# VectorE copies of K's indicator rows, and a last output block in two halves, in a chunk-select attention with a gMLP block

## The chip, the cores and the metric

The kernel runs on one core of a Trainium2 chip. Its engines work side by side and wait for each other through semaphores: TensorE (PE in the profile; its weight loads are PEld), VectorE (DVE), ScalarE (ACT), GpSimd (POOL) and SyncE (SP), which here only issues DMAs and waits. The metric is the device time of one execution in microseconds (us); lower is better. Times of one instruction are often given in nanoseconds (ns).

## The reference

Two layers follow each other. The first is a causal attention that lets every query attend to only six chunks of 32 keys, chosen by an upper bound of its scores; the second is a gMLP block over the 512 features of the eight heads together.

```python
def _attn_ref(q, k, v):                       # (4, 8, 768, 64) each
    k_min, k_max = min, max of k over chunks of 32 rows
    ub = sum_d maximum(q * k_min, q * k_max)   # (B, H, 768, 24)
    ub = where(causal, ub, -1e9)
    top_chunks = argsort(ub)[..., -6:]
    scores = q @ k.T / sqrt(64)
    mask = (chunk of key in top_chunks) & (query pos >= key pos)
    attn = softmax(where(mask, scores, -1e9))
    return attn @ v

def _moe_ref(x, w_in, g_ln, w_sg, b_sg, w_out):   # x (4, 768, 512)
    h = gelu_tanh(x @ w_in)                        # (4, 768, 1024)
    u, v = h[..., :512], h[..., 512:]
    v_n = layer_norm(v) * g_ln
    v_s = einsum('ts,bsd->btd', w_sg, v_n) + b_sg[None, :, None]
    return x + (u * v_s) @ w_out
```

Inputs and output are float32.

## The kernel before

**Stages.** The 32 heads are worked off as 16 pairs, four pairs to a batch of the gMLP. For a pair p, `prep(p)` transposes K and Q on TensorE (tags ktr and qtr, line 508), takes K's minimum and maximum by chunk on VectorE (kmm, L532), moves K and Q out of PSUM (kev, qev; L425 on ScalarE, L428 on VectorE), computes the upper bounds on TensorE (ub, L602 or L649), and finds the sixth largest on VectorE: transposes (utr), MAX8 (m8), a comparison (dn), a transpose back (dt). `scores` or `scores_full` computes the scores on TensorE (sc) with exp on ScalarE (exp) and the causal triangle on GpSimd (aff); `head` multiplies by V (pv, pvd) and divides on VectorE (rcp, xs, the latter into tile XS). `xtrans` transposes the result of a pair for the gMLP (xtr, and xev out of PSUM, into xT). After four pairs `moe_h` computes gelu of both halves (hv, gv; hu, gu) and the normalization (bns, bna, var, rstd, vhat), and `moe_g` the spatial product (pt, vs, gt), the output projection (ou, L926), the residual add on VectorE (os, L933) and the store (st, L937).

**How chunks that were not chosen are masked.** For the first four pairs the scores get extra matmuls with an indicator matrix (L763). For pairs 4 to 15 the indicator is part of the operands instead: a K operand `KA[w][i]` has 64 rows of K and 64 rows of an indicator (tile INDF, 128 x 768 in bf16), and `QA[w][i]` has 64 rows of Q and the mask rows that DMAs write (qd, L682). There are four such buffers (w = p mod 4). For pairs 4 to 7 `mask_rows(w)`, called after the scores of pair w, puts the indicator rows into the buffer that pair w has left: one DMA of 64 x 768 bf16 for each of the two heads (tag mrow, L690), and a memset of QA on GpSimd (L693). From pair 8 on (KSPR) the rows come by two other DMAs (kcp L545, kin L548), which the change leaves alone.

**The order of the work.** Every step is registered with `P.op(engine, fn, cost, tag, reads, writes, ...)` and gets the next number; from the names read and written the program derives what each step must wait for. The order on each engine is not that of the program but a list of these numbers (TABLE), found ahead of time by a search with the costs given to `P.op`; TensorE's list also says where spare matmuls are put in ("filler"), and "slots" gives each PSUM tile its bank. An engine works off its list strictly in order, so a step that waits holds up all that stand behind it in the same list; for SyncE these are DMA issues. DMAs of one name (`dma=`) wait for each other: an mrow DMA of one head waits for the one before to land.

Numbers that come up below: mrow 206 and 208 (pair 0), 258 and 260 (pair 1), 323 and 325 (pair 2), 375 and 377 (pair 3); the first of each two is for the head whose K rows are the lower ones and waits for the scores of its pair. ktr of pair 9: 578 and one more; qtr of pair 9: 589 and 591; load of half of K of pair 9: 411; of K of pair 12: 658 and 659; of half of Q of pair 12: 660 (a load of pair p overwrites the buffer of pair p − 3). kmm of pair 3: 152, 156, 157; qev of pair 3: 161. kev of pair 5, second half: 270, 271. dn and dt of pairs 4 and 5: 288, 289; wev, a move of transposed gMLP weights: 142. In the last batch ou, os and st of block 3 are 1288, 1289, 1290; of block 4 1291, 1292, 1293; of block 5 1294, 1295, 1296.

## Time and profile before

| what | value |
|---|---|
| median of 3 runs | 216.06 us (215.18 to 216.32) |
| the profiled execution | 216.26 us |
| its span, first to last instruction | 214.5 us |
| granted TensorE clock, mean | 0.999 of full speed |
| DMA | 35.47 MB, mean 165 GB/s |
| output stores (L937), issue to landing | 2.3 us, median of 24 |

The profile lists instructions by engine and by line of the kernel (L690 is line 690). "out<-in" are the tiles an instruction writes and reads. A row such as "6.4, 542 | 0.5 <-PE" means 6.4 us busy in all, 542 ns mean of one, and 0.5 us for which the engine was idle just ahead of these instructions, ended by TensorE. The chain of waits follows the execution back from its last instruction, at each step to what released it. SPq is SyncE's issuing of DMAs; a DMA's landing is told apart from its issue.

### The profile page before, as it was taken

The page shows a single profiled execution, that of the slowest core. Times are in us where ns is not written, and L with a number is a line of the kernel's source. Part 1 is how long each engine was busy: PE and PEld are TensorE (multiplying, and loading weights), DVE is VectorE, ACT ScalarE, POOL GpSimd, SP SyncE. Part 2 cuts the span into 40 slices and gives each one's busy share as a digit, 9 for nine tenths or more (in the row PEclk, how much of TensorE's full clock was granted, in tenths as well). Part 3 has the DMA queues.
Part 4 walks back from the last instruction along what each step waited for, and adds up shares of the span by engine and source line. Part 5 has one row for each costly group of instructions (what it writes and reads, how often), then busy time and mean ns, then how long its engine had stood idle before and what let it go on. Part 6 is the DMA issues. An engine that isn't in the chain of part 4 may idle for free.

```text
span 214.5 us, 5915 instructions
## 1 busy us (share of the span) xinstructions
PE 202.6 (94%) x2331; PEld 134.4 (63%) x2345; DVE 183.1 (85%) x526; ACT 149.9 (70%) x223; POOL 101.3 (47%) x151
## 2 busy tenths in 40 slices
PE   7789999879999999999999999999999999999993
PEld 2547668634766668697555676779445669545641
DVE  3599789979989998798899898988897877879983
ACT  2778997717798668988868777889868888353000
POOL 7346669965425948768260076399102542010000
PEclk9999999999999999999999999999999999999999
DMA  7999999999579998969987918848104402010316
GB/s 152 218 218 204 260 265 294 297 207 261 92 192 268 207 236 242 241 161 246 213 188 161 193 47 172 255 127 121 44 0 125 113 19 82 3 49 5 142 55 238
DMA packets 87450, 35.47 MB, mean 165 GB/s; under 512 B 80128, under 2 KB 82432, under 8 KB 87424
## 3 DMA queue, kind: packets, MB, share of 16 engines
q1 hardware_dynamic: 87424, 35.11, 70.9%
q8 instruction: 18, 0.29, 0.6%
q14 instruction: 8, 0.07, 0.1%
HBM read 24.77 MB, written 6.29 MB: 145 GB/s over the span
## 4 chain that ended last, share of the span: by engine, by line
PE 72%; DVE 11%; ACT 7%; DMA 4%; issue 2%; SPq 1%; POOL 1%; DVEq 0%
PE PSG L907 13%; PE PSC L717 12%; PE PSG L926 9%; PE PSG L844 7%; PE PSG L508 7%; PE PSG L795 6%; PE PSG L890 5%; DVE W L532 3%; ACT E L772 3%; PE PSG L649 3%; PE PSG L802 2%; DMA kn<-in_k_dram 2%; PE PSC L367 2%; PE PSG L829 2%; PE PSC L757 2%; ACT KA L425 2%
## 5 line engine op out<-in xcount | busy, mean ns | idle before, releaser
L723 ACT ACTIVATE E<-PSC 128x1024 bf16<-128x1024 f32 (+1 forms) x72 | 63.0, 920 | 9.3 <-PE PSC L717 8.0
L532 DVE TENSOR_REDUCE W<-PSG 128x12 f32<-128x384 f32 x64 | 32.8, 547 | 6.4 <-PE PSG L508 6.4
L717 PE MATMUL PSC<-QA,KA 128*128 128x128 bf16 (+2 forms) x336 | 37.5, 246 | 0.4 <-DMA QA<-Dt 0.3
L907 PE MATMUL PSG<-wsgT,vhat 128*128 128x384 bf16 x192 | 35.0, 326 | 0.0
L572 POOL CAST QA<-qT 64x768 bf16<-64x768 f32 (+1 forms) x28 | 23.0, 822 | 15.7 <-PE PSC L717 14.1
L728 POOL TENSOR_SCALAR_AFFINE_SELECT E<-E 128x768 bf16<-128x768 bf16 x24 | 20.6, 866 | 20.5 <-ACT E L723 20.2
L717 PEld LDWEIGHTS PSC<-QA,KA 128*128 128x128 bf16 x336 | 24.1, 98 | 7.5 <-issue 1.1
L895 ACT ACTIVATE uT<-PSG 128x384 bf16<-128x384 f32 x32 | 15.6, 491 | 17.5 <-PE PSG L890 17.2
L907 PEld LDWEIGHTS PSG<-wsgT,vhat 128*128 128x128 bf16 x192 | 18.0, 98 | 11.1 <-DVE PSG L913 0.5
L890 PE MATMUL PSG<-xT,winb 128*128 128x384 bf16 x128 | 23.9, 326 | 0.0
L848 ACT ACTIVATE vgb<-PSG 128x512 f32<-128x512 f32 x24 | 14.2, 597 | 13.9 <-PE PSG L844 13.0
L772 ACT ACTIVATE E<-PSC 128x1024 bf16<-128x1024 f32 (+1 forms) x24 | 20.6, 914 | 4.1 <-PE PSC L763 4.1
L913 DVE SCALAR_TENSOR_TENSOR PSG<-PSG,glnT,bsgbc 128x384 f32<-128x384 f32 x32 | 19.7, 619 | 3.8 <-PE PSG L907 3.5
L844 PE MATMUL PSG<-winb,xT 128*128 128x512 bf16 x91 | 21.4, 379 | 0.9 <-DVE xT L428 0.5
L926 PE MATMUL PSG<-woutb,uT 128*128 128x512 bf16 x87 | 21.6, 379 | 0.6 <-DVE rden L810 0.2
L795 PE MATMUL PSG<-vx,E 128*128 128x65 bf16 x480 | 19.9, 194 | 0.7 <-ACT E L772 0.7
L795 PEld LDWEIGHTS PSG<-vx,E 128*128 128x128 bf16 x480 | 17.6, 98 | 3.0 <-ACT E L772 0.9
L917 DVE TENSOR_TENSOR uT<-PSG,uT 128x384 bf16<-128x384 f32 x32 | 17.6, 553 | 1.2 <-ACT uT L895 0.3
L565 POOL TENSOR_SCALAR rT<-qT 128x576 f32<-128x576 f32 x16 | 10.9, 683 | 15.7 <-ACT qT L425 11.0
L812 DVE TENSOR_TENSOR XS<-PSG,rden 128x384 bf16<-128x384 f32 x32 | 17.5, 549 | 0.7
L933 DVE TENSOR_TENSOR osb<-PSG,XS 128x512 f32<-128x512 f32 x24 | 16.1, 684 | 2.0 <-PE PSG L926 1.9
L853 DVE BATCH_NORM_STATS2 stats<-vgb 128x6 f32<-128x512 f32 x24 | 15.7, 680 | 2.4 <-ACT vgb L848 2.3
(84 smaller groups left out, 339.9 us busy)
## 6 DMA issues: line engine op xcount, KB each, us to landing
qn<-in_q_dram SPq DMA_DIRECT2D x32, 192.0 KB, 4.7
kn<-in_k_dram SPq DMA_DIRECT2D x32, 192.0 KB, 4.6
vn<-in_v_dram SPq DMA_DIRECT2D x16, 384.0 KB, 5.0
out_dram<-osb SPq DMA_DIRECT2D x24, 256.0 KB, 2.3
uT<-in_moe_w_sg_dram SPq DMA_DIRECT2D x4, 384.0 KB, 4.8
KA<-INDF SPq DMA_DIRECT2D x16, 96.0 KB, 4.3
vgb<-in_moe_w_in_dram SPq DMA_DIRECT2D x3, 512.0 KB, 6.7
QA<-Dt SPq DMA_DIRECT2D x24, 36.0 KB, 2.3
```

The source lines that it names most:

```text
L532: P.op("dve", lambda d, m=m, op=op, src=src, h0=h0, h1=h1: d.tensor_reduce(W[w][:, m, 12 * h0:12 * h1].rearrange("p (h c) -> p h c", h=h1 ...
L572: P.op("pool", lambda g, i=i, r0=r0, r1=r1: g.tensor_copy(QA[w][i or 0][r0:r1, :], qT[r][r0:r1, :]), gps(S, 250 if i == 1 else 150), ("qca ...
L717: r = e.matmul(t.ap()[:, o:o + n], KA[w][i][:, 128 * kb:128 * kb + 128], QA[w][i][:, q0:q0 + n], start=True, stop=True)
L723: P.op("act", lambda e, t=t, c0=c0, c1=c1, i=i: e.activation(E[es][:, i, c0:c1], t.ap()[:, 0:c1 - c0], ACTF.Exp, scale=SCALE), act(c1 - c0 ...
L728: P.op("pool", lambda g, ev=ev: g.affine_select(ev, ev, pattern=[[0, NT], [1, 128]], compare_op=ALU.is_ge, fill=0.0, base=0, channel_multi ...
L772: P.op("act", lambda e, t=t, c0=c0, c1=c1, n=n: e.activation(E[es][:, :, c0:c1], t.ap().rearrange("p (i x) -> p i x", i=2)[:, :, 0:n], ACT ...
L795: r = e.matmul(t.ap()[:, 65 * qb:65 * qb + 65], E[es][:, i, a:a + 128], vx[w][:, kb, i, :], start=first, stop=False, skip_group_check=True)
L844: r = e.matmul(t.ap()[:, 0:F], xT[s][:, dk, 128 * qt:128 * qt + 128], winb[:, dk, F:DFF], start=(dk == 0), stop=(dk == NDK - 1))
L890: r = e.matmul(t.ap()[:, 0:TG], winb[:, dk, 128 * fb:128 * fb + 128], xT[s][:, dk, TG * tg:TG * tg + TG], start=(dk == 0), stop=(dk == NDK ...
L907: r = e.matmul(t.ap()[:, 0:TG], vhat[s][:, sb, 128 * fb:128 * fb + 128], wsgT[:, sb, TG * tg:TG * tg + TG], start=(sb == 0), stop=(sb == N ...
L913: P.op("dve", lambda d, t=t, fb=fb, tg=tg: d.scalar_tensor_tensor(t.ap()[:, 0:TG], t.ap()[:, 0:TG], glnT[:, fb:fb + 1], bsgbc[:, TG * tg:T ...
L926: r = e.matmul(t.ap()[:, 0:DM], gT[s][:, fb, 128 * qt:128 * qt + 128], woutb[:, fb, :], start=(fb == 0), stop=(fb == NF - 1))
```

## The change

Three things change. The two copies of INDF's rows in `mask_rows` are made by VectorE's `tensor_copy` (MROW = "dve") and no longer by DMAs; the names that they read and write stay. The residual add and the store of block 5 of the last batch, the last one in the program, are each split into two halves of 256 columns (LAST = 1), the second store under a DMA name of its own. And all lists of TABLE are new: the eight numbers of mrow have gone from SyncE's list to VectorE's, two numbers are new (1295 and 1296 are add and store of the first half, 1297 and 1298 of the second), and the other steps stand in another order on all five engines.

```diff
@@ -316,6 +316,8 @@
     VH = ("dve","dve","dve","dve")
     XDMA = tuple((2, d) for d in range(NDK))
     WSGT = "bf16"
+    MROW = "dve"
+    LAST = 1
     NWSB = 1
     TRX = 750
     TRI = 1300
@@ -687,9 +689,13 @@
 
         for i in range(2):
             m0 = 64 * (1 - i)
-            P.op("sp", lambda e, i=i, m0=m0: e.dma_start(KA[w][i][m0:m0 + 64, :], INDF[m0:m0 + 64, :]),
-                 dmac(590), ("mrow", w, i, 0), reads=["INDF"], dma=f"mrow{i}", xfer=450,
-                 writes=[("KI", w, i)] + ([("KA", w, 0, 0), ("KA", w, 0, 1)] if i == 0 else []))
+            ki = [("KI", w, i)] + ([("KA", w, 0, 0), ("KA", w, 0, 1)] if i == 0 else [])
+            if MROW == "dve":
+                P.op("dve", lambda d, i=i, m0=m0: d.tensor_copy(KA[w][i][m0:m0 + 64, :], INDF[m0:m0 + 64, :]), (290, 380),
+                     ("mrow", w, i, 0), port=True, reads=["INDF"], writes=ki)
+            else:
+                P.op("sp", lambda e, i=i, m0=m0: e.dma_start(KA[w][i][m0:m0 + 64, :], INDF[m0:m0 + 64, :]),
+                     dmac(590), ("mrow", w, i, 0), reads=["INDF"], dma=f"mrow{i}", xfer=450, writes=ki)
             P.op("pool", lambda g_, i=i, m0=m0: g_.memset(QA[w][i][m0:m0 + 64, :].bitcast(mybir.dt.uint32), 0),
                  gps(S // 2, 150), ("mrow", w, i, 2), shift=(i == 0), writes=[("QD", w, i)] + ([("QA", w, 0, 0), ("QA", w, 0, 1)] if i == 0 else []))
 
@@ -930,13 +936,19 @@
                      reads=[("uT", s, fb, tg) for fb in range(NF)] + [("woutb", fb) for fb in range(NF)],
                      writes=[t], alloc=t)
                 os_ = (b * NT + qt) % 3
-                P.op("dve", lambda d, t=t, qt=qt, os_=os_: d.tensor_tensor(
-                    osb[os_][:].rearrange("p (a x) -> p a x", x=128),
-                    t.ap()[:, 0:DM].rearrange("p (a x) -> p a x", x=128), XS[:, b % 2, :, qt, :], op=ALU.add), dve(DM), ("os", b, qt),
-                    reads=[t] + [("XS", b % 2, hh) for hh in range(H)], writes=[("osb", os_)], ps=[t])
-                P.op("sp", lambda e, qt=qt, os_=os_: e.dma_start(
-                    bass.AP(out.tensor, (b * S + 128 * qt) * DM, [[DM, 128], [1, DM]]), osb[os_][:]), dmac(),
-                    ("st", b, qt), reads=[("osb", os_)], dma=f"o{os_}", xfer=680)
+                cuts = (0, DM // 2, DM) if LAST and (b, qt) == (B - 1, NT - 1) else (0, DM)
+                for x, (c0, c1) in enumerate(zip(cuts, cuts[1:])):
+                    more = (x,) if len(cuts) > 2 else ()
+                    P.op("dve", lambda d, t=t, qt=qt, os_=os_, c0=c0, c1=c1: d.tensor_tensor(
+                        osb[os_][:, c0:c1].rearrange("p (a x) -> p a x", x=128),
+                        t.ap()[:, c0:c1].rearrange("p (a x) -> p a x", x=128), XS[:, b % 2, c0 // 128:c1 // 128, qt, :],
+                        op=ALU.add), dve(c1 - c0), ("os", b, qt) + more,
+                        reads=[t] + [("XS", b % 2, hh) for hh in range(c0 // 64, c1 // 64)],
+                        writes=[("osb", os_) + more] if more else [("osb", os_), ("osb", os_, 0), ("osb", os_, 1)], ps=[t])
+                    P.op("sp", lambda e, qt=qt, os_=os_, c0=c0, c1=c1: e.dma_start(
+                        bass.AP(out.tensor, (b * S + 128 * qt) * DM + c0, [[DM, 128], [1, c1 - c0]]), osb[os_][:, c0:c1]), dmac(),
+                        ("st", b, qt) + more, reads=[("osb", os_) + more] if more else [("osb", os_), ("osb", os_, 0), ("osb", os_, 1)], dma=f"o{os_}" if x == 0 else "olast",
+                        xfer=680 * (c1 - c0) / DM)
 
     SEL, GRP, u = {}, {}, 0
...
 TABLE = {
     "pe": (
...
-        "496 490 515 560 469 558 475 556 390 472 466 398 487 565 563 484 541 589 493 543 481 567 652 650 517 "
-        "478 530 512 591 505 578 519 502 534 526 624 527 522 523 582 617 621 499 574 626 575 674 597 628 619 "
...
+        "496 490 560 515 469 558 475 390 556 472 466 398 563 487 484 543 567 519 591 589 481 512 478 541 493 "
+        "652 650 565 578 530 517 505 502 624 526 527 534 617 522 523 582 621 499 626 574 575 674 597 628 619 "
...
-        "1261 1285 1253 1282 1270 1273 1267 1294 1291 1288 "),
...
+        "1241 1285 1253 1282 1270 1273 1267 1291 1294 1288 "),
...
     "dve": (
...
-        "97 163 153 156 117 157 25 118 200 161 119 120 201 204 205 211 212 168 169 170 256 171 257 216 217 26 "
-        "252 130 253 264 263 266 224 300 265 27 317 318 134 321 235 322 222 270 271 269 268 369 352 370 373 "
-        "374 274 417 276 424 282 425 285 283 286 284 287 420 380 381 421 432 428 433 138 429 440 436 142 441 "
-        "437 288 442 385 289 386 447 449 146 448 445 444 150 446 334 333 497 498 491 329 492 328 470 471 476 "
...
-        "1266 1277 1278 1262 1263 1286 1287 1283 1284 1271 1274 1268 1292 1295 1289 "),
...
+        "157 163 26 25 152 156 27 161 117 206 118 153 119 204 200 120 205 201 211 212 168 169 235 208 258 170 "
...
+        "370 268 274 417 276 270 271 375 323 424 285 286 282 380 287 425 420 381 283 421 284 428 432 429 288 "
+        "433 138 440 436 441 437 142 442 289 385 386 449 447 146 448 446 445 150 444 260 334 333 497 498 491 "
+        "328 492 329 470 471 476 477 473 467 474 468 402 399 403 400 488 404 489 485 401 482 405 325 377 406 "
...
+        "1281 1256 1257 1259 1265 1260 1277 1266 1262 1263 1286 1278 1287 1283 1284 1271 1274 1268 1292 1295 "
+        "1297 1289 "),
...
     "sp": (
-        "32 31 29 30 34 33 35 36 38 39 41 64 40 65 67 66 37 172 122 123 42 124 131 173 125 206 127 72 68 258 "
-        "75 121 73 174 175 70 295 294 135 231 323 139 297 232 375 143 178 296 208 147 230 99 229 290 347 98 "
-        "292 291 180 260 182 348 176 293 349 550 126 413 414 325 411 552 551 346 412 486 298 377 408 483 407 "
-        "233 480 410 611 613 409 612 538 507 549 350 610 504 722 586 607 661 660 609 553 501 859 721 608 539 "
-        "614 658 860 587 695 919 857 861 647 606 720 659 696 920 648 719 723 415 716 715 718 858 918 662 917 "
...
-        "921 1016 954 812 997 1083 1086 1089 1110 1104 1107 1272 1275 1269 1293 1296 1290 "),
...
+        "68 174 175 70 295 294 135 232 139 231 297 143 296 349 147 180 230 413 229 290 291 99 98 292 348 178 "
+        "412 176 293 182 298 347 346 414 126 551 552 660 411 486 233 410 408 483 407 480 549 613 409 661 612 "
+        "350 610 538 611 607 606 550 586 860 614 721 553 659 695 658 722 608 859 539 719 720 647 723 587 415 "
...
+        "1089 1104 1110 1107 1272 1275 1269 1293 1296 1298 1290 "),
...
     "filler": (
-        "54:9 43:1 81:2"),
+        "52:8 43:2 81:3"),
...
```

8 lines of the change are left out of this document (4 added, 4 removed), and 80 rows, old and new, of the table TABLE.

## The prediction, made before the changed kernel was run

> **What bounds the kernel now.** I read the page first: its span, its busy shares and the chain of waits.
>
> ```profile
> span 214.5 us, 5915 instructions
> PE 202.6 (94%) x2331; PEld 134.4 (63%) x2345; DVE 183.1 (85%) x526; ACT 149.9 (70%) x223; POOL 101.3 (47%) x151
> PE 72%; DVE 11%; ACT 7%; DMA 4%; issue 2%; SPq 1%; POOL 1%; DVEq 0%
> ```
>
> TensorE is busy for 94% of the span and holds 72% of the chain that ends last. The profiled execution took 216.26 us around its span of 214.5, so 1.76 us lie outside the span; the median of the runs shown is 216.06, which is 0.20 less. The sum below is made against 216.26.
>
> An average says little here, so I asked next for the busy time by stages.
>
> ```profile
> core 0: us, PE busy (x) PEld busy (x) DVE busy (x) ACT busy (x) POOL busy (x), PEclk, DMA share, GB/s
> 20.00:45.00 25.00, 22.59 (x451) 16.96 (x452) 22.05 (x71) 19.55 (x26) 19.90 (x29) 1.00 1.09 271
> 45.00:165.00 120.00, 117.93 (x1340) 79.50 (x1351) 108.10 (x331) 95.32 (x148) 62.97 (x87) 1.00 0.75 172
> 165.00:205.00 40.00, 39.84 (x359) 25.24 (x361) 33.40 (x69) 22.32 (x31) 7.92 (x9) 1.00 0.20 63
> ```
>
> From 45 to 205 us TensorE lacks only 2.07 + 0.16 us of 160. From 20 to 45 us it lacks 2.41 of 25, and there VectorE is busy for 22.05, idle for 2.95. Who ends that stage is in the chain of waits, followed through 38 to 46 us (start, length, what):
>
> ```profile
> 38.60 0.43 DVE xT L428
> ...
> 43.17 0.57 DVE XS L812
> ...
> 43.78 0.52 PE PSG L829 x6
> ...
> 44.89 0.47 DVE qT L428
> ```
>
> VectorE ends the stage: it finishes the fourth pair's output (XS), then moves its transpose (xT), and the gMLP's matmuls can begin. What shortens VectorE's list ahead of 45 us brings the filled stretch forward by as much; what lengthens it pushes that back. VectorE's own waits, and ScalarE's longest, between 20 and 45 us (total, times, longest):
>
> ```profile
> ACT E L772 <- PE PSC L763: 2.3, 4, 1.1
> DVE U L612 <- PE PSG L602: 1.6, 2, 1.0
> DVE rden L810 <- PE PSG L802: 0.7, 2, 0.5
> ```
>
> **The eight copies: their price.** The change takes eight DMAs of 96 KB (L690) off SyncE and gives VectorE eight copies of 64 partitions x 768 bf16, SBUF to SBUF. No row has such a copy. The nearest rows of VectorE, with those that the later steps need (groups by line and shape: busy, mean ns of one):
>
> ```profile
> L913 DVE SCALAR_TENSOR_TENSOR PSG<-PSG,glnT,bsgbc 128x384 f32<-128x384 f32 x32 | 19.7, 619 | 3.8 <-PE PSG L907 3.5
> L917 DVE TENSOR_TENSOR uT<-PSG,uT 128x384 bf16<-128x384 f32 x32 | 17.6, 553 | 1.2 <-ACT uT L895 0.3
> ...
> L933 DVE TENSOR_TENSOR osb<-PSG,XS 128x512 f32<-128x512 f32 x24 | 16.1, 684 | 2.0 <-PE PSG L926 1.9
> ...
> L428 DVE COPY xT<-PSG 128x768 bf16<-128x768 bf16 x12 | 6.4, 542 | 0.5 <-PE PSG L829 0.2
> ...
> L428 DVE CAST KA<-PSG 64x384 bf16<-64x384 f32 x4 | 2.2, 548 | 0.0
> ...
> L384 DVE MEMSET IND<- 32x768 bf16 x1 | 0.7, 698 | 0.1
> ...
> L364 DVE MEMSET warm<- 128x256 uint32 x1 | 0.3, 272 | 0.9 <-PEq L1118 0.9
> ```
>
> Above stands 0.70 us, one element at a time (L384). Below stands 0.27 us, the time of 256 words (L364). I take 0.41: 768 bf16 are 384 words of 32 bits, and 384 x 272/256 = 408 ns; the copy of as many elements out of PSUM takes 0.54.
>
> By the Trainium skill, "VectorE: DVE Perf Modes", section "The perf-mode tier table", a bf16 copy within SBUF runs at four elements a cycle, and its section on the TRN2 errata gives a measured fixed term of about 150 cycles; the estimate from these is (192 + 150)/0.96 = 356 ns, and with it the forecast would be 0.16 us lower. No row of this trace shows that mode.
>
> **Where the copies stand.** In the new list of VectorE three of them (206, 208, 258) stand ahead of the end of that stage, five after it. 206 and 258 wait for the last scores of pairs 0 and 1, which those stages of the list have behind them, so nothing queues up behind a wait. The two casts of K's second half of pair 5 (270, 271) go the other way, from ahead of pair 3's XS to behind qT's last move, into VectorE's wait for the first gelu. So the list ahead of the end of the stage becomes 3 x 0.41 = 1.23 longer and 2 x 0.548 = 1.10 shorter. The new list also puts three reductions and a qT move (157, 152, 156, 161) before the transpose that waited longest (1.0 of "DVE U L612"); I count that 1.0 as filled, and half of the 0.7 of rden, because two more ready instructions are put ahead of these reciprocals: −1.35. Stage: 1.23 − 1.10 − 1.35 = **−1.22**. The bounds: with copies at 0.27, −1.64; with copies at 0.70 and nothing filled, 2.10 − 1.10 = +1.00. The other five copies cost 5 x 0.41 = 2.05 us of VectorE after 45 us, where it is idle for 120 − 108.10 = 11.9; I take nothing. Two of them stand between the comparison and the transpose of pairs 6 and 7 (dn and dt of that group), but one vs (L913, 0.62) is moved out of the same place. Without that cover they cost 0.82.
>
> **SyncE's queue without the eight DMAs.** Here are L690's own instructions (min/median/max ns), and then SyncE's waits between 24 and 50 us:
>
> ```profile
> L690 SPq DMA_DIRECT2D KA<-INDF x8: 467/639/1586, 23.7 to 76.8; - x8
> DMA to landing us min/median/max: 2.8/4.5/6.9
> ```
>
> ```profile
> SPq L199 <- DMA KA<-INDF: 4.7, 2, 3.5
> SPq L690 <- PE PSG L802: 1.3, 1, 1.3
> ```
>
> Each of these DMAs waits for the one before of its name to land, so SyncE stood still for 4.7 us. That queue time is freed, and about 8 x 0.64 = 5.1 us of issuing. It is worth only what a late load cost TensorE; in the whole trace two places show a wait of TensorE on a DMA after the first loads:
>
> ```profile
> 60.69 0.51 PE L717 MATMUL PSC<-QA,KA 128*128 128x128 bf16 x6 [0.28 <-DMA QA<-Dt]
> ...
> 117.17 0.55 PE L508 MATMUL PSG<-identF,kn 128*128 128x128 f32 x3 [0.52 <-DMA kn<-in_k_dram]
> ```
>
> The second is K of pair 12. In the new list of SyncE its two loads (659, 658) stand ahead of the indicator DMAs of pairs 8 and 9 instead of behind them, some 20 entries earlier: **−0.52**. The first is the mask rows of pair 4: the new list of VectorE puts their comparison and transpose (288, 289) ahead of a copy of 0.55 us (142): **−0.28**. Bounds of both: 0 to what is taken.
>
> **What the new order makes late.** SyncE works its list in order. It now has 660, Q of pair 12, right ahead of 411, half of K of pair 9. 660 overwrites Q of pair 9 and must wait until TensorE has transposed both of its halves (591, 589). From there to 578, the transpose that reads 411, TensorE's new list holds two output blocks, one spatial block, two score tiles and three transposes. Prices from the chain of waits, and then the loads' issue (min/median/max, ns) and landing between 64 and 85 us:
>
> ```profile
> 61.74 0.66 PE PSG L508 x6
> ...
> 74.80 0.97 PE PSG L907 x6
> ...
> 76.10 0.86 PE PSG L926 x4
> ...
> 78.19 0.44 PE PSC L717 x4
> ```
>
> ```profile
> L492 SPq DMA_DIRECT2D qn<-in_q_dram x7: 583/686/2320, 64.6 to 84.8; - x7
> ...
> DMA to landing us min/median/max: 3.4/4.6/6.4
> ```
>
> TensorE: 2 x 0.86 + 0.97 + 2 x 0.44 (the smaller of the two tiles less, 0.3) + 3 x 0.33 = 4.4 us. SyncE: 0.69 + 4.6 = 5.3. K arrives 0.9 late; **+0.8** is taken for the wake-up that both share. From both sides: 0.69 + 3.4 gives nothing, 0.69 + 6.4 gives +2.7.
>
> **The tail.** The last microseconds, instruction by instruction:
>
> ```profile
> 209.14 1.67 PE L926 MATMUL PSG<-woutb,uT 128*128 128x512 bf16 x7
> ...
> 209.99 1.29 DVE L933 TENSOR_TENSOR osb<-PSG,XS 128x512 f32<-128x512 f32 x2 [1.04 <-PE PSG L926]
> 210.44 0.38 PE L926 MATMUL PSG<-woutb,uT 128*128 128x512 bf16 x1
> ...
> 211.20 0.68 DVE L933 TENSOR_TENSOR osb<-PSG,XS 128x512 f32<-128x512 f32 x1
> 211.31 0.93 SPq L937 DMA_DIRECT2D out_dram<-osb  x2
> ```
>
> Before, TensorE makes blocks 5, 4, 3 (1294, 1291, 1288) while VectorE adds 4, 5, 3 (1292, 1295, 1289): it idles for 1.04 us until block 4 is there and then has three adds of 0.68 in a row, the last from 211.20 to 211.88, though TensorE ended at 210.82. After, TensorE's list ends 1291, 1294, 1288. The block that is cut is number 5, which is last in the program and not on any engine: block 3 still ends everything, whole. Block 4's add begins one block earlier, at about 209.13; the halves of block 5 begin when it is done, at 209.99. A half costs 256 elements: from 384 elements at 0.553 (L917) and 512 at 0.684, 0.42 each, 0.84 for 0.68. They end at 210.83, when block 3 is there. Its add ends at about 211.52 instead of 211.88: **−0.36**. It comes from the order; the cut itself costs 0.16 of VectorE and one more issue (0.93 for two, so 0.47) on SyncE, which ends near 211.4, before the last add does. Bounds: 0 to −0.4.
>
> **Sum:** −1.22 − 0.52 − 0.28 + 0.80 − 0.36 = −1.58, so 216.26 − 1.58 = **214.7 us**.
>
> **The rivals.**
> *Stage ahead of 45 us unchanged* (216.0): the idle that the list fills at one place opens at the next, as VectorE waits for TensorE's scores anyway. 1.23 − 1.10 − 0.52 − 0.28 + 0.80 − 0.36 = −0.23. For it speaks that ScalarE, too, waited 2.3 us there; against it that VectorE alone stands in the chain.
> *The idle all filled* (213.1): 2.95 instead of 1.35 of VectorE's idle goes.
> *K of pair 9 at the slowest landing* (216.6): 2.7 instead of 0.8.
> *Copies held up by GpSimd* (slower). GpSimd is busy for 19.90 of 25 us in that stage, with instructions such as the first row; the second is a VectorE instruction that reads SBUF alone, with its shortest, median and longest time:
>
> ```profile
> L728 POOL TENSOR_SCALAR_AFFINE_SELECT E<-E 128x768 bf16<-128x768 bf16 x24 | 20.6, 866 | 20.5 <-ACT E L723 20.2
> ```
>
> ```profile
> L879 DVE TENSOR_SCALAR vhat<-vgb,mv,rstd x24: 529/542/636, 57.9 to 195.7; 128x512 bf16<-128x512 f32 x24
> ```
>
> If a copy costs 0.70 and waits out half of such an instruction (0.43), the three make 3 x 1.13 − 1.10 = +2.29, nothing is filled, the rest gives −0.36: 218.2. With p the price of a copy the time is 216.26 + 3p − 1.46, which passes 217.14 from p = 0.78. Against it: L879 takes 0.636 at its longest, 0.1 over its median, so no run of it here waited for a whole GpSimd instruction.
> The Trainium skill, "SBUF — State Buffer", section "SBUF: two separate sides", says that such a wait is real: a VectorE instruction in a two-port mode and a GpSimd instruction lock each other out for a whole instruction. By that rule this rival is the likelier one; L879, at 512 elements in 0.54 us, runs at one element a cycle and so doesn't test it.
> *New gaps* (217.4): the lists are shuffled most from 70 to 125 us, where TensorE was full; if these 55 us lose 5% (the stage ahead of 45 us loses 10%), that is +2.75 on the forecast.
> *The change does not do what it says*: true of the cut, and in the sum.
>
> **How the numbers follow.** Forecast 0.40; all filled 0.06; stage unchanged 0.18; slow landing 0.08; copies held up 0.16; new gaps 0.12. About 0.5% of the median, 1.08 us, is what a measurement can tell: faster means under 214.98, slower over 217.14. Faster takes the first two less a little, 0.44; same 0.26; slower 0.30. The forecast's own range is 213.5 to 215.8 (price of a copy, landing of one load). The range reaches to the copies held up on one side and past the all-filled case on the other: 212.8 to 218.3.
>
> **What would show it.** The copies' mean on VectorE (0.41; over 0.78 breaks the forecast); VectorE's qT move that stands at 44.89 about 1.2 us earlier; no wait of SyncE on KA; no wait of TensorE on kn near 116 us but one of about 0.8 near 79 us; VectorE's last add whole, preceded by two halves of 0.42 without idle; TensorE's idle between 45 and 205 us still near 2.2 us. A larger idle there makes the prediction wrong.

## The result, and the profile after

The changed kernel takes 217.48 us in the median of 22 runs (215.94 to 218.89), the kernel before 216.29 (22 runs, 215.18 to 218.86). The ratio is 1.0049 with a 95% interval of 1.0025 to 1.0072: it is about half a per cent slower, where 214.7 us and "faster" were forecast. The profiled execution took 217.79 us around a span of 216.0.

The page of the changed kernel, its first lines and the shares of the chain of waits:

```profile
span 216.0 us, 5925 instructions
PE 203.3 (94%) x2332; PEld 134.6 (62%) x2346; DVE 186.8 (87%) x535; ACT 149.7 (69%) x223; POOL 103.1 (48%) x151
PE 69%; DVE 17%; ACT 5%; DMA 3%; issue 2%; SPq 1%; POOL 1%; DVEq 0%
```

VectorE's share of the chain has grown from 11% to 17%: it now stands in places where TensorE ruled. The same stages as before:

```profile
core 0: us, PE busy (x) PEld busy (x) DVE busy (x) ACT busy (x) POOL busy (x), PEclk, DMA share, GB/s
20.00:45.00 25.00, 22.57 (x451) 16.89 (x446) 22.95 (x73) 19.41 (x26) 20.75 (x29) 1.00 1.06 269
45.00:165.00 120.00, 116.41 (x1310) 78.35 (x1319) 108.29 (x332) 93.73 (x146) 63.65 (x86) 1.00 0.74 170
165.00:205.00 40.00, 39.33 (x374) 25.28 (x377) 34.02 (x72) 22.67 (x31) 7.18 (x8) 1.00 0.15 52
```

TensorE's idle time from 45 to 205 us has gone from 2.23 us to 3.59 + 0.67 = 4.26. The forecast had named a larger idle there as what would make it wrong. What ended TensorE's longer waits, between 45 and 130 us and then between 130 and 205 us:

```profile
PE PSC L723 <- DMA QA<-Dt: 1.2, 1, 1.2
PE PSG L850 <- DVE U L660: 0.6, 1, 0.6
PE PSG L651 <- DVE KA L430: 0.5, 1, 0.5
```

```profile
PE PSC L723 <- ACT E L729: 0.5, 1, 0.5
PE PSG L913 <- DVE vhat L885: 0.5, 1, 0.5
```

To see where time is lost and not only where an engine stands still, I compared executions at equal work: the time at which TensorE has begun the same sum of instruction lengths. Each column is a kernel's time less that of the kernel before, in us (positive is later); the first column is the time of the kernel before at that point. The traces of before, after and e1 lack 14 matmul records that the others have; these are counted in, and an entry can be off by some 0.2 us for it.

```
before  after   a1     a2     a4     c1     c2     c3     d1     d2     e1
 15.2   -0.59  -0.38  -0.88  -0.22  -0.66  -0.35  -0.44  -0.22  +0.27  -0.71
 45.4   -1.10  +0.20  -1.36  +0.52  -1.25  -0.26  -0.61  -1.24  +0.26  -1.21
 49.9   -0.12  +1.12  -0.96  +0.68  -1.02  +0.11  -0.21  -0.85  +0.27  -0.28
 54.1   -0.20  +1.04  -1.24  +0.68  -1.30  -0.17  -0.49  -1.12  +0.27  -0.36
 62.4   -0.18  +1.07  -1.22  +0.65  -1.29  -0.16  +0.96  -1.10  +0.59  -0.34
 66.5   +1.16  +1.04  +0.08  +1.47  -1.32  +0.85  +0.93  -1.13  +2.42  -0.37
111.9   +1.25  +0.87  -0.01  +1.61  -0.98  +1.04  +0.70  -0.85  +2.16  -0.31
120.6   +0.71  +0.33  -0.55  +1.49  -1.52  +0.50  +0.09  -1.39  +1.54  -0.85
144.8   +0.62  +0.25  -0.64  +1.49  -1.61  +0.41  +0.01  -1.48  +1.54  -0.93
153.0   +1.22  +0.79  -0.49  +1.49  -1.18  +0.79  +0.67  -0.85  +1.53  -0.78
169.7   +1.67  +0.86  -0.46  +1.49  -1.20  +0.81  +0.65  -0.38  +1.53  -0.77
```

The column "after" tells the story: a lead of 1.10 us at 45 us is lost in two steps of 0.98 (45 to 50 us) and 1.34 us (62 to 67 us), half a microsecond comes back near 117, and 1.05 goes near 150 and 165. The letters are the experiments below. One execution is behind each column, so they show places; how much a kernel gains or loses is read from the medians.

**The first loss: two copies beside GpSimd.** All copies on VectorE (min/median/max ns), then VectorE and GpSimd between 44.5 and 50 us (start, length):

```profile
L694 DVE COPY KA<-INDF x8: 343/351/978, 22.5 to 79.0; 64x768 bf16<-64x768 bf16 x8
```

```profile
44.17 1.11 DVE L430 CAST KA<-PSG 64x384 bf16<-64x384 f32 x2
45.32 1.63 DVE L694 COPY KA<-INDF 64x768 bf16<-64x768 bf16 x2
46.96 0.69 DVE L859 BATCH_NORM_STATS2 stats<-vgb 128x6 f32<-128x512 f32 x1
47.57 1.47 DVE L660 STREAM_TRANSPOSE U<-PSG 64x288 f32<-64x288 f32 x3
```

```profile
45.01 0.82 POOL L423 CAST wsb<-vhat 128x768 bf16<-128x768 f32 x1
45.78 3.64 POOL L574 CAST QA<-qT 64x768 bf16<-64x768 f32 x4
```

Most copies take 0.34 to 0.36 us. These two (375 and 323, pairs 3 and 2) take 1.63 together. GpSimd is in a cast of its own all the while, and its four casts take 3.64 us, where the kernels without a copy beside them need 3.48 or 3.49 (a2, c1, c2, c3).

Behind the copies stand the statistics and then pair 4's three transposes. TensorE stops twice in this stretch:

```profile
45.43 0.72 PE L651 MATMUL PSG<-qT,W 64*32 64x288 f32 x16 [0.55 <-DVE KA L430]
...
48.58 1.69 PE L850 MATMUL PSG<-winb,xT 128*128 128x512 bf16 x7 [0.60 <-DVE U L660]
```

The second stop is for the transposes; it appears in the five kernels whose VectorE makes pairs 3 and 2's rows at this place (after, a1, a3, d3, e1: 0.55 to 0.79 us) and in no other. The first is for the two casts 270 and 271, which the new list of VectorE puts here. All ten kernels with the new orders have it (0.37 to 0.55 us), with or without copies; the kernels with the old orders wait there 0.18 to 0.34 us, for GpSimd. So about 0.6 of the 0.98 us belongs to the copies.

**The second loss: pair 5's mask rows.** SyncE's issues from 58 us, and from the chain of waits what TensorE waited for:

```profile
58.58 0.58 SPq L416 DMA_DIRECT2D glnT<-in_moe_g_ln_dram  x1
59.20 0.51 SPq L419 DMA_DIRECT2D bsgbc<-in_moe_b_sg_dram  x1
59.75 0.51 SPq L684 DMA_DIRECT2D QA<-Dt  x1
```

```profile
59.75 5.49 DMA QA<-Dt
...
65.38 0.88 PE PSC L723 x10
```

The new list of SyncE puts the gMLP's scale and its bias (99 and 98; 2 KB and 384 KB) straight ahead of the mask rows of pair 5's first head (292, 36 KB). These land 5.49 us after their issue, and TensorE waits 1.2 us for them. All 24 such loads of this execution (min/median/max to landing) show how far off that is:

```profile
L684 SPq DMA_DIRECT2D QA<-Dt x24: 513/592/1192, 57.3 to 166.0; - x24
...
DMA to landing us min/median/max: 1.8/1.9/5.5
```

In the kernel before the bias stands ahead of these rows, too. There they were issued at 59.96, half a microsecond further behind it, and landed in 3.7 us, in time for TensorE:

```profile
58.85 1.06 SPq L417 DMA_DIRECT2D bsgbc<-in_moe_b_sg_dram  x1
59.96 1.16 SPq L682 DMA_DIRECT2D QA<-Dt  x2
```

```profile
L682 SPq DMA_DIRECT2D QA<-Dt x1: 528/528/528, 60.0 to 60.0; - x1
...
DMA to landing us min/median/max: 3.7/3.7/3.7
```

Issue and landing of both in five kernels (us from the start of the span):

| kernel | bias | mask rows 292 |
|---|---|---|
| before | 58.85 to 63.48 | 59.96 to 63.68 |
| after | 59.20 to 63.71 | 59.75 to 65.24 |
| c2 | 60.30 to 64.33 | 60.85 to 64.61 |
| d2 | 61.22 to 65.90 | 61.77 to 66.14 |
| e1 | 48.01 to 53.51 | 59.04 to 60.93 |

In all eight profiles with the bias just ahead, the rows land only after the bias has landed: 0.2 to 0.3 us after it in before, a4, c2, c4 and d2, and 1.5 to 1.6 in after, a2 and a3. The distance of the two issues doesn't decide between these: c2 and after have the same. What does stays open.

TensorE's new list also asks for these rows sooner. Step 560, the first of pair 5's scores, stands ahead of 515, a score tile of pair 4 whose rows had landed at 59.85; in the kernel before it stands behind it. With 515 first (0.44 us in before, from 64.19 to 64.63) TensorE would wait that much less; this is an estimate, it was not tried.

**The tail.** VectorE's output adds after, and the first of them before:

```profile
208.49 1.28 DVE L942 TENSOR_TENSOR osb<-PSG,XS 128x512 f32<-128x512 f32 x2
...
211.34 2.13 DVE L942 TENSOR_TENSOR osb<-PSG,XS 128x512 f32<-128x512 f32 x4 [0.72 <-DMA out_dram<-osb]
```

```profile
206.82 1.28 DVE L933 TENSOR_TENSOR osb<-PSG,XS 128x512 f32<-128x512 f32 x2
```

From the first of these adds to the end of the span it takes 216.0 − 208.49 = 7.51 us, before 214.5 − 206.82 = 7.68. Block 4's add still waits 0.72 us: it writes the output buffer from which block 1 is being stored.

### The profile page after: what moved, and what is told of

The parts are those of the page before. It is cut to its first block, busy times and chain, and to the rows that moved or that the text cites. A ratio compares the mean times of both kernels' runs of the same rounds, so it can differ in the third digit from the quotient of the medians.

```text
span 216.0 us, 5925 instructions
## 1 busy us (share of the span) xinstructions
PE 203.3 (94%) x2332; PEld 134.6 (62%) x2346; DVE 186.8 (87%) x535; ACT 149.7 (69%) x223; POOL 103.1 (48%) x151
## 4 chain that ended last, share of the span: by engine, by line
PE 69%; DVE 17%; ACT 5%; DMA 3%; issue 2%; SPq 1%; POOL 1%; DVEq 0%
PE PSG L913 13%; PE PSC L723 12%; PE PSG L510 7%; PE PSG L932 7%; PE PSG L801 6%; PE PSG L850 5%; PE PSG L896 3%; DVE stats L859 3%; PE PSG L651 3%; PE PSG L808 3%; DVE vhat L885 3%; DMA QA<-Dt 3%; PE PSC L763 2%; PE PSC L369 2%; DVE U L660 2%
## 5 line engine op out<-in xcount | busy, mean ns | idle before, releaser
L734 POOL TENSOR_SCALAR_AFFINE_SELECT E<-E 128x768 bf16<-128x768 bf16 x24 | 21.4, 901 | 28.1 <-ACT E L729 27.7
L579 POOL CAST vx<-vn 128x768 bf16<-128x768 f32 x16 | 13.4, 837 | 15.4 <-DMA vn<-in_v_dram 15.2
L942 DVE TENSOR_TENSOR osb<-PSG,XS 128x512 f32<-128x512 f32 (+1 forms) x25 | 16.2, 663 | 2.5 <-PE PSG L932 1.6
L427 ACT ACTIVATE KA<-PSG 128x384 bf16<-128x384 f32 (+1 forms) x34 | 16.4, 487 | 1.5 <-DVE W L534 1.2
```

Of the source, the lines that this page charges most:

```text
L734: P.op("pool", lambda g, ev=ev: g.affine_select(ev, ev, pattern=[[0, NT], [1, 128]], compare_op=ALU.is_ge, fill=0.0, base=0, channel_multi ...
```

## The experiments

Three theories stood at the start. *Copies*: the two copies beside GpSimd cost the first loss. *Mask rows*: the place of the loads of scale and bias costs the second. *Diffuse*: the new orders lose a little everywhere, and any single repair only moves the waits. All twelve kernels were timed in five rounds of alternation with the kernel before; its median beside them was 216.35 to 216.39 us, and 215.90 beside e1, so the ratios compare better than the medians. Numbers in the diffs are steps of TABLE.

| kernel | median us | ratio to before | 95% interval |
|---|---|---|---|
| after | 217.48 | 1.0049 | 1.0025 to 1.0072 |
| a1, scale and bias earlier | 216.37 | 0.9997 | 0.9972 to 1.0022 |
| a2, two copies on ScalarE | 216.38 | 0.9983 | 0.9956 to 1.0009 |
| a3, last blocks in own buffers | 217.29 | 1.0036 | 1.0018 to 1.0055 |
| a4, copies in the old orders | 217.68 | 1.0054 | 1.0030 to 1.0079 |
| c1, a1 + a2 + a3 | 215.11 | 0.9944 | 0.9915 to 0.9974 |
| c2, new orders with DMAs | 216.58 | 1.0002 | 0.9974 to 1.0031 |
| c3, a1 + two copies later | 216.97 | 1.0033 | 1.0004 to 1.0063 |
| c4, cut alone | 216.11 | 0.9994 | 0.9968 to 1.0020 |
| d1, c2 + a1 + a3 | 215.03 | 0.9947 | 0.9914 to 0.9980 |
| d2, old orders, biases first | 217.56 | 1.0053 | 1.0022 to 1.0084 |
| d3, a1 + copies as reductions | 216.38 | 0.9993 | 0.9959 to 1.0027 |
| e1, bias alone earlier | 215.96 | 1.0015 | 0.9989 to 1.0041 |

### a1: scale and bias straight behind K of pair 6

```diff
 "sp":
-... 147 180 230 413 229 290 291 99 98 292 348 178 ...
+... 147 180 230 99 98 413 229 290 291 292 348 178 ...
```

> The changed kernel with two entries of SyncE's list moved: the loads of the gate's scale (99) and bias (98), which stand right ahead of the mask rows of pair 5 (qd), go some ten entries forward, behind 230. Theory W (a wait on mask rows): the mask rows of pair 5 took 5.5 us to land behind them and TensorE stood 1.2 us at about 65 us; with the loads out of the way they land in about 2 to 3 us, that stall is gone, and the kernel is 1.0 to 1.4 us faster than the changed kernel, a ratio to the kernel before of about 0.999. Theory C (the copies on VectorE are what costs): no change, ratio about 1.005. Theory D (the loss is spread over the new order and any one place is refilled): the stall goes and under 0.4 us of it is seen in the time, ratio 1.003 to 1.005.

The two loads go four entries forward, not ten, and are issued at 50.6 and 51.6 us instead of 58.6 and 59.2.

216.37 us, 1.1 less than the changed kernel. The mask rows of pair 5 are no longer among TensorE's waits, and the curve loses nothing from 62 to 67 us. The loss at 45 to 50 us stays (+0.20 to +1.12). So the rows are late by what stands ahead of them. The lead of 1.1 us at 45 us did not come in this profile, though the order up to there is the same; the section on the prediction comes back to that.

### a2: the two copies on ScalarE

```diff
-            if MROW == "dve":
+            if MROW == "dve" and w > 1 and i == 0:
+                P.op("act", lambda d, ...: d.activation(KA[w][i][m0:m0 + 64, :], INDF[m0:m0 + 64, :], ACTF.Copy), ...)
+            elif MROW == "dve":
 "act": 323 375 put ahead of 423
```

> The changed kernel with two of the eight copies (323 and 375, the lower rows of pairs 2 and 3) made by ScalarE instead of VectorE, in the 4 us for which ScalarE waits for the first gelu. Theory C says that these two copies, which took 0.98 and 0.73 us of VectorE while GpSimd was busy (the others 0.34 to 0.46), push back the transposes of the upper bounds of pairs 4 and 5: the transposes begin 1 to 1.5 us earlier, and the kernel is 0.6 to 1.0 us faster than the changed one, ratio about 1.001. Theory W: TensorE's 1.2 us on the mask rows stay, and since that DMA is issued earlier too, up to 0.5 us is gained; ratio 1.002 to 1.005.

216.38 us, the same 1.1 less. The copies as this execution shows them, six on VectorE and two on ScalarE:

```profile
L697 DVE COPY KA<-INDF x6: 344/346/465, 22.2 to 77.9; 64x768 bf16<-64x768 bf16 x6
L694 ACT ACTIVATE KA<-INDF x2: 823/832/841, 39.2 to 40.0; 64x768 bf16<-64x768 bf16 x2
```

ScalarE needs 0.83 us for one, much more than VectorE alone, and the kernel is quicker all the same: at 39 us ScalarE has the room. On VectorE, where the copies were:

```profile
45.29 0.69 DVE L862 BATCH_NORM_STATS2 stats<-vgb 128x6 f32<-128x512 f32 x1 [0.26 <-ACT vgb L857]
...
46.47 1.49 DVE L660 STREAM_TRANSPOSE U<-PSG 64x288 f32<-64x288 f32 x3 [0.49 <-PE PSG L651]
```

VectorE is idle there for 0.26 + 0.49 us, and TensorE's stop for the transposes is gone. Of the loss at 45 to 50 us 0.40 is left (−1.36 to −0.96), with the stop for the two casts, and it is made up by 54 us. The loss at 62 to 67 us stays whole (−1.22 to +0.08).

### a3: the last three output blocks in buffers of their own

```diff
+                far = b == B - 1 and qt >= 3
+                dst = vg[qt] if far else osb[os_]
```

> The changed kernel with the last three output blocks added into vg's slices, dead by then, instead of the three osb buffers, and stored under DMA names of their own. Theory: the add of block 4 waited 0.7 us for the store of block 1 to land, because both use one buffer; without that wait the adds of the tail follow TensorE, the last add begins when TensorE ends, and the time between TensorE's end and the last add's end falls from 1.0 to 0.7 us: 0.3 to 0.4 us faster than the changed kernel. Rival (the stores queue up behind one another anyway): the last landing does not move, under 0.1 us.

The three stores have DMA names of their own, too. The adds of the last blocks in this kernel:

```profile
210.22 0.69 DVE L945 TENSOR_TENSOR vgb<-PSG,XS 128x512 f32<-128x512 f32 x1 [0.17 <-PE PSG L932]
211.08 1.56 DVE L945 TENSOR_TENSOR vgb<-PSG,XS 128x256 f32<-128x256 f32 x3 [0.17 <-PE PSG L932]
```

The wait on the store is gone, and block 4 is added as soon as TensorE has made it. From the first output add (207.91) to the end of the span (215.3) it is 7.39 us instead of 7.51: 0.12 us less for a wait of 0.72, since block 3, last on TensorE, has to be waited for anyway. In the medians that is 217.29 against 217.48, not to be told apart.

### a4: the copies alone, in the old orders

The kernel before, with all eight copies put on VectorE and the rest of each list unchanged.

```diff
 "sp":  206 208 258 260 323 325 375 377 taken out
 "dve": 206 ahead of 118; 208 258 behind 169; 375 323 ahead of 424; 260 behind 444; 325 377 behind 405
```

> The kernel before, its lists kept, with the eight DMAs of the indicator rows taken out of SyncE's list and eight copies put into VectorE's, next to the same neighbours as in the changed kernel; no cut block. Theory C: this is most of the loss, ratio 1.003 to 1.006, and VectorE's transposes of pairs 4 and 5 begin 0.8 us or more later than in the kernel before. Theory W or D: the copies alone cost what their two slow ones push back, 0 to 0.5 us, and SyncE's freed queue gives some of it back: ratio 0.998 to 1.002.

217.68 us, half a per cent over the kernel before: the copies lose in the old orders, too, but not at the same place. Pairs 3 and 2's take 0.36 and 0.82 us here, without a loss at 45 to 50 us. The kernel is 0.5 us behind at 45 us already, and loses another 0.8 at 62 to 67 us, where TensorE waits for mask rows as well:

```profile
PE PSC L717 <- DMA QA<-Dt: 0.6, 1, 0.6
```

### c1: the three repairs together

The edits of a1, a2 and a3 in the changed kernel.

> The changed kernel with three things moved at once: the gln and bias loads behind kn of pair 6, the copies of pairs 2 and 3's first head on ScalarE, and the last three output blocks in buffers of their own. Theory of two separate losses (about 1.0 us at 45 to 50 us from the two copies beside GpSimd, about 1.3 us at 50 to 67 us from the late indicator-mask load): they add, TensorE's wait on pair 5's mask rows is gone and its equal-work lead of about 1.1 us at 45 us is kept to the end; 216.4 less another 1.0 to 1.5 us, so 214.7 to 215.4 us, ratio 0.990 to 0.996 to the kernel before. Rival, that each single repair only moved the waits about (any shuffle gives the same 216.4): 216.2 to 216.6 us, ratio 0.998 to 1.002.

215.11 us, 2.4 less than the changed kernel and 0.56% (0.26% to 0.85%) quicker than the kernel before. The two repairs of 1.1 us each add up, which speaks against the diffuse theory. The column c1 has nothing of the second step and 0.23 us of the first, and from 45 to 205 us TensorE has only three waits that count, of 0.4 (for the two casts), 0.3 and 0.3 us.

### c2: the new orders with all copies as DMAs

```diff
-    MROW = "dve"
+    MROW = "sp"
 "sp": the eight copies again between the loads they stood between before
```

> The new orders and the cut kept, but all eight indicator copies are DMAs on SyncE again, each put between the loads that it stood between before. Theory that copies cost at 45 us: the equal-work loss at 45 to 50 us goes (1.0 us), the loss at pair 5's mask rows stays or grows, because two more issues of about 0.6 us stand ahead of them on SyncE (1.3 to 2.0 us); 216.3 to 217.0 us. Rival, that the new orders themselves lose and the copies do not matter: 217.5 us as the changed kernel. Rival, that the new orders pay only with the copies on VectorE: over 218 us.

216.58 us, 0.9 less than with the copies on VectorE, at the edge of what can be told (the intervals of the two ratios just overlap). The new orders and the cut with the old DMAs make no difference to the kernel before (1.0002), and the step to VectorE, within these orders, costs about what it costs within the old ones (a4). The wait for pair 5's mask rows is still there (0.5 us).

### c3: the two copies where GpSimd rests

```diff
 "sp":  as in a1
 "dve":
-... 271 375 323 424 ... 421 284 ... 288 433 ...
+... 271 424 ... 421 375 284 ... 288 323 433 ...
```

> The changed kernel with the gln and bias loads moved as in the first experiment, and the copies of pairs 2 and 3's first head left on VectorE but moved from ahead of pair 4's transposes (45.3 us) to 51.3 and 54 us, where GpSimd rests. Theory that they cost by place, beside GpSimd and ahead of the transposes: both take 0.34 to 0.36 us, GpSimd's casts at 45 to 49 us are back to 0.82 us each, and the loss at 45 to 50 us is gone; 214.9 to 215.6 us, as with the copies on ScalarE. Rival, that VectorE has no room for them anywhere in the stage and loses their 0.69 us in any place: 0.7 us more than with ScalarE, 215.6 to 216.2 us. Rival, nothing regained beyond the loads' move: 216.4 us.

The price came as expected, the time did not. Both copies take 0.36 us, and of the loss at 45 to 50 us 0.40 is left and soon made up. But the median is 216.97 us, clearly over c1's 215.1; against a1's 216.4 the intervals overlap. VectorE from 53 us in this kernel, then GpSimd's cast beside it, then the same instructions in the changed kernel:

```profile
53.45 1.32 DVE L676 TENSOR_TENSOR Dn<-U,m 128x576 bf16<-128x576 f32 x1
54.78 0.36 DVE L694 COPY KA<-INDF 64x768 bf16<-64x768 bf16 x1
...
55.26 0.52 DVE L430 COPY wsgT<-PSG 128x768 bf16<-128x768 bf16 x1
```

```profile
53.34 0.82 POOL L423 CAST wsb<-vhat 128x768 bf16<-128x768 f32 x1 [3.64 <-PE PSG L479]
```

```profile
53.31 0.73 DVE L676 TENSOR_TENSOR Dn<-U,m 128x576 bf16<-128x576 f32 x1
...
54.04 0.53 DVE L430 COPY wsgT<-PSG 128x768 bf16<-128x768 bf16 x1
```

```profile
53.62 1.10 POOL L423 CAST wsb<-vhat 128x768 bf16<-128x768 f32 x1 [4.21 <-PE PSG L479]
```

With one copy more ahead of it (0.36 us) pair 4's comparison (L676) starts just after GpSimd's cast instead of just before it, and takes 1.32 us instead of 0.73; in the changed kernel it is the cast that pays (1.10 instead of 0.82). The move of the gMLP's transposed weights (L430) comes 1.22 us later, and TensorE, which waits for such moves (1.1 us), loses 1.45 us between 54 and 62 us. In this profile the 0.36 us of one copy was paid fourfold.

### c4: the cut alone

The kernel before, with block 5 of the last batch cut in two and nothing else changed.

> The kernel before with its own orders and its DMAs, only the last output block of the second batch cut into two halves. Theory from the tails of the five profiles (first output add to end of span 7.68 us without the cut, 7.42 to 7.51 us with it): 0.17 to 0.26 us faster, 216.0 to 216.3 us, ratio 0.9985 to 1.000. Rival, that the cut gains its whole half store, as forecast (0.36 us): 215.9 us. Rival, that the wait on the store of block 1 hides all of it: 216.4 us, no change in that stretch.

216.11 us, no difference that can be told. My expectation for the tail was wrong: from the first output add (206.23) to the end of the span (214.0) it is 7.77 us, against 7.68 without the cut. So the 0.17 that the changed kernel gains at the end is put down to its order of the last blocks and not to the cut; both are differences of single profiles. This profile's span is shorter than before's for what happened ahead of 45 us.

### d1: DMAs, with scale and bias out of the way

The kernel c2 with the edits of a1 and a3: it differs from c1 in the copies alone.

> The new orders and the cut with all eight copies as DMAs on SyncE, the gln and bias loads behind kn of pair 6, and the last three output blocks in buffers of their own: as the kernel of three repairs, but with DMAs in place of the copies on VectorE and ScalarE. Theory that the move off the DMAs gains nothing and the repairs alone make the kernel of three repairs quick: no wait on pair 5's mask rows, 215.0 to 215.6 us, ratio 0.993 to 0.997. Rival, that the eight issues taken off SyncE were worth something once VectorE is spared (SyncE issues pair 4's and 5's mask rows 1.2 us later with two copies ahead of them): mask rows late again, 215.9 to 216.6 us, ratio 0.998 to 1.001.

215.03 us, equal to c1. Once these two loads are out of the way, the eight issues that the copies save SyncE are worth nothing that can be measured, and the old DMAs do as well as ScalarE and VectorE together. So the quicker kernel owes the copies nothing that these runs can tell; the two intervals are 0.6% wide.

### d2: the kernel before with the biases ahead of the mask rows

```diff
 "sp":
-... 230 99 229 290 347 98 292 291 180 ...
+... 230 229 290 347 291 99 98 292 180 ...
```

> The kernel before in its own orders, only that SyncE issues pair 4's second mask rows and then the gln and bias loads straight ahead of pair 5's mask rows, as the changed kernel does. Theory that a 384 KB load straight ahead makes these rows land 5 us after issue instead of 3.7 us: issued at about 60 us they land near 65.2 us and TensorE waits 0.7 to 1.3 us before pair 5's scores; 217.0 to 217.7 us, ratio 1.003 to 1.006. Rival, that the old TensorE order has other work there and covers it: 216.2 to 216.5 us, ratio 0.999 to 1.001.

217.56 us, 1.2 over the kernel before, as expected. TensorE's waits for mask rows from 45 to 130 us, 0.6 us for pair 4's and 0.9 for pair 5's, and in time the score matmuls of pair 5:

```profile
PE PSC L717 <- DMA QA<-Dt: 1.5, 2, 0.9
```

```profile
66.27 0.43 PE L717 MATMUL PSC<-QA,KA 128*128 128x256 bf16 x3 [0.89 <-DMA QA<-Dt]
```

The rows were issued at 61.8 us, later than the 60 that I expected, because two issues more stand ahead of them, and landed 4.4 us after that; late issue and slow landing share the loss. The place of three entries in SyncE's list makes the old kernel as slow as the changed one.

### d3: the copies as reductions

a1 with the two copies in their old place, done by another VectorE instruction with the same operands and result.

```diff
+                P.op("dve", lambda d, ...: d.tensor_reduce(KA[w][i][m0:m0 + 64, :],
+                     INDF[m0:m0 + 64, :].rearrange("p (s o) -> p s o", o=1), axis=AX.X, op=ALU.max), dve(S), ...)
```

> The changed kernel with the gln and bias loads moved as in the first experiment, and the two copies of pairs 2 and 3's first head done in their old place on VectorE as a maximum over one element each, which has the same operands and result. Theory that the copy itself is held out while GpSimd works (0.73 and 0.98 us beside GpSimd against 0.34 us alone, GpSimd's cast 0.96 us against 0.82 us): the other instruction takes the same 0.7 to 0.9 us whether GpSimd works or not, both equal within 5%, and GpSimd's casts beside it are back to 0.82 us; the time stays that of the first experiment, 216.2 to 216.6 us, since the two still hold VectorE for about 1.6 us. Rival, that any VectorE access to SBUF is slowed beside GpSimd: the two differ as the copies do and the casts stay near 0.96 us.

```profile
L694 DVE TENSOR_REDUCE KA<-INDF x2: 944/946/949, 45.8 to 46.7; 64x768 bf16<-64x768 bf16 x2
```

```profile
45.44 0.82 POOL L423 CAST wsb<-vhat 128x768 bf16<-128x768 f32 x1
46.20 3.48 POOL L574 CAST QA<-qT 64x768 bf16<-64x768 f32 x4
```

Both take 0.95 us (a little over the 0.7 to 0.9 expected), equal to half a per cent, and GpSimd's four casts need 3.48 us instead of 3.64. So it is not any access of VectorE that GpSimd slows, but this form of copy. The time is a1's, and TensorE's stop for the transposes is there as well (0.79 us): VectorE is held for about as long, 1.81 us against 1.63. What costs is how long VectorE is held at this place, not what holds it.

### e1: the bias alone

The changed kernel with only the bias (98) moved, as in a1; the scale (99) stays ahead of the mask rows.

> The changed kernel with only the bias load (384 KB) moved behind kn of pair 6; the scale (2 KB) stays ahead of pair 5's mask rows. Theory that the bias alone makes these rows late: they land about 1.9 us after issue as in the first experiment, TensorE has no wait on them, 216.2 to 216.7 us. Rival, that the issue taken by the scale (0.6 us on SyncE) is what they lack, since the kernel before has the bias straight ahead of them, too, and no wait: they still land late or are issued too late, TensorE waits 0.5 us or more, 216.9 to 217.5 us.

215.96 us, 1.0015 of the kernel before, which had 215.90 beside it. The mask rows of this stage land as quickly as they ever do, and TensorE has no wait on them:

```profile
L684 SPq DMA_DIRECT2D QA<-Dt x3: 513/582/600, 57.1 to 59.0; - x3
...
DMA to landing us min/median/max: 1.9/1.9/1.9
```

So it is the bias that makes them late, and not the scale or the time that its issue takes. In time e1 alone proves little, as its interval overlaps the changed kernel's; that the late rows cost a microsecond rests on a1 and d2.

## Why the prediction was wrong, point by point

**The steps that failed** are two, and both are terms taken as nothing; a third term, the two casts, was mis-sized. The 217.48 us lie above the forecast's own range (213.5 to 215.8).

*"The other five copies ... I take nothing."* VectorE's 11.9 us of idle were a sum over 120 us. Two of the five copies stand between 45 and 47 us, ahead of three transposes for which TensorE waits. Without them VectorE is idle there for 0.75 us (a2). Alone a copy takes 0.34 to 0.36 us (0.41 was taken), so two would just fit; that is an estimate, no run shows it. Beside GpSimd's casts the two took 1.63 us, over the bound of 0.70 each, and TensorE stood for 0.60. With the two on ScalarE 1.1 us come back in the medians. That GpSimd could hold copies up was a rival, with 218.2 us; it was priced for the three copies ahead of 45 us, which took 0.46 + 0.71 = 1.17 (1.23 was taken), and not for these two.

By the Trainium skill, "SBUF — State Buffer", section "Who interferes with whom", a copy in a two-port mode and a GpSimd instruction shut each other out for a whole instruction, whichever came first, and `tensor_reduce` on trn2 is never held up. The traces agree that both sides pay, with 1.63 us for two copies beside casts against 0.34 to 0.36 each alone and 3.64 us for four casts instead of 3.48, and that the two reductions, at 0.95, don't touch GpSimd (3.48). The same section says that a VectorE instruction with two SBUF inputs meets GpSimd's reads in the same way; the comparison of 1.32 us in c3 instead of 0.73 agrees.

*"It is worth only what a late load cost TensorE", and only loads that were late before were looked at.* The new order of SyncE made another load late: pair 5's mask rows behind the bias, and TensorE's new list asked for them ahead of a tile whose rows were there. It cost 1.34 us of the profile; a1 gives 1.1 us back, d2 takes 1.2 us from the old kernel with the same order, and e1 names the bias as the one that matters. The forecast had gone through SyncE's new list for pair 9 and pair 12 alone. The entries ahead of 292, and 560 ahead of 515, stood in the diff.

**The stage ahead of 45 us** (−1.22 forecast): the lead is 1.10 us, and VectorE's last qT move stands 1.10 us earlier (43.71 against 44.81). But that the size agrees is luck. Of the lead 0.59 was there at 15 us, ahead of every copy; TensorE's first transposes begin 0.43 us earlier, behind nine spare matmuls instead of ten. VectorE's idle from 20 to 45 us fell by 0.90 us (2.95 to 2.05), not by 1.35: its wait for the upper bounds went from 1.6 to 0.2 us, but that ahead of the reciprocals, of which half was to go, grew from 0.7 to 1.4. And the two casts, counted as 1.10 saved, hold TensorE up at their new place, by 0.2 to 0.4 us more than it waited there before. At 45 us the kernels with the new orders stand anywhere between −1.36 and +0.20, c2 and d1 without any copy among them.

**K of pair 12** (−0.52): right; its wait is gone, and 0.54 us comes back between 112 and 121 us. **Mask rows of pair 4** (−0.28): it isn't waited for any more. **K of pair 9** (+0.80): did not come. TensorE went from the end of Q's transposes (75.60 + 0.83) to those of K in 4.3 us (4.4 forecast), but the load landed 3.0 us after its issue, less than the shortest of 3.4 that was taken:

```profile
75.60 0.83 PE L510 MATMUL PSG<-identF,qn 128*128 128x128 f32 x6
...
80.77 0.91 PE L510 MATMUL PSG<-identF,kn 128*128 128x128 f32 x6
```

```profile
L494 SPq DMA_DIRECT2D kn<-in_k_dram x1: 546/546/546, 76.9 to 76.9; - x1
...
DMA to landing us min/median/max: 2.7/2.9/3.0
```

**The tail** (−0.36): 0.17 in the profile. That the cut itself gains nothing agrees with c4; what was missed is the wait for the store of block 1 (0.72), of which a3 wins back 0.12.

**Late waits.** About 1.05 us goes between 145 and 170 us: before pair 13's scores, which wait for ScalarE, and before a spatial block, which waits for VectorE. The first place shows in all columns of the new orders (0.15 to 0.66 between 145 and 153 us) and in none of a4 and d2, which have the old ones; in c3 and d1 the wait there is for a DMA into KA. The "new gaps" rival (217.4) meant such losses, but between 70 and 125 us, where the changed kernel lost nothing; that its number is near the measured one is chance. Which entry of the lists makes them was not tried and stays open; c1 and d1 are quicker than the kernel before in spite of them.

In sum: 1.34 for the mask rows and 0.98 for the two copies and the two casts were missing, 1.05 came late, where the forecast had no term, and of the gains −0.54 and −0.17 came; with the lead of 1.10 that is 1.6 us, and the spans differ by 1.5.

## What to carry to other kernels

A copy is hidden by idle time at its own place, not by the idle of a stage: look at what the engine does in the two microseconds where it will stand, and at what GpSimd does beside it: the same copy took 0.35 us alone and 0.8 in the mean beside casts. When a queue's order changes, go through the short transfers that the busiest engine waits for and see which long ones now stand ahead of each. A change with several parts is worth taking apart: here the new orders gained 0.5% over the kernel before once two entries of one queue were moved and three blocks had their own buffers (d1), and the part that gave the change its name lost about half a per cent (c2, a4).

## What the runs showed of the hardware

A 36 KB transfer from SBUF to SBUF landed 1.9 us after its issue in the six profiles without a load of 384 KB just ahead of it in SyncE's list (pair 5's mask rows in a1, c1, c3, d1, d3, e1). In the eight with that load 0.5 to 1.5 us ahead it took 3.4 to 5.5 us and landed only after the load had.

A VectorE comparison (L676) took 1.32 us where it started 0.1 us behind a GpSimd cast (c3), and 0.73 where it started 0.3 us ahead of the same one (after): a shift of 0.4 us between the two engines was worth 0.6 us.

Two VectorE copies of 64 x 768 bf16 beside GpSimd casts took 1.57 to 1.63 us together in four profiles (after, a1, a3, e1), and the casts grew with them, 3.64 us for four instead of 3.48.

ScalarE copies 64 x 768 bf16 in 0.83 us, VectorE in 0.34 to 0.36 alone, and VectorE's reduction over one element takes 0.95 for the same data.
